# Weight loads of 128 rows of 8 KB, a buffer of its own for w1, and q loads ahead of w2's blocks, in a fused soft-capped attention and maxout kernel

## The chip, the cores and the metric

The kernel runs on one core of one Trainium2 chip, as one launch. The metric is the device time in microseconds (us). Three runs of the kernel before took 338.31, 339.49 and 340.12 us; the median is 339.49 us. The profile is of one execution, recorded by the hardware profiler.

## The reference

Attention over 8 batches of 12 heads, 448 positions, head size 64, with the scores capped by a tanh, then a layer that takes the larger of two projections and projects it back:

```python
scores = cap * np.tanh(scale * np.matmul(q, k.transpose(0, 1, 3, 2)) / cap)
attn = np.exp(scores - max(scores)); attn = attn / sum(attn)
x = (attn @ v).transpose(0, 2, 1, 3).reshape(3584, 768)
h1 = x @ w1            # w1, w2: 768 x 1024, w_out: 1024 x 768
h2 = x @ w2
out = np.maximum(h1, h2) @ w_out
```

All inputs and the output are float32 in HBM.

## The kernel before

The kernel works in bf16 on chip. It rewrites the second layer: max(h1, h2) is h2 + relu(h1 - h2), so the output is x (w2 w_out) + relu(x (w1 - w2)) w_out. Two weight tiles are therefore made on chip in the first 55 us: `wd_sb` = w1 - w2 by six subtractions ("sub", L377), and `wm_sb` = w2 w_out by matmuls ("P", L403) that need w2 turned ("W", 16 or 8 transposes on TensorE at L388, copied to `w2T` at L392 by "WC").

The six row chunks of w1 and w2 are numbered 0 to 5. Chunk 2m + u holds, on partition p, row 256 m + 2 p + u of the matrix. Each chunk is a load of its own, of 128 rows of 4 KB in HBM that lie 8 KB apart. The chunks of w2 go to `w2b`, a view of the buffer that later holds `gT`, and are cast to bf16 on the way ("lw2", L368). The chunks of w1 stay float32 ("lw1", L374): 0 to 3 go to the four output buffers `osb`, 4 and 5 to a view of one of the two `xT` buffers. w_out comes in four quarters `wo_sb` ("lwo half part", L359): `half` picks 384 output columns, `part` picks four of the eight row blocks f.

The work of attention goes by 48 pairs of heads, i = 0 to 47, and two pairs share a step t = i // 2. "lk i", "lq i" and "lv t" load k, q and v (L322 for i under 10, L329 after that, L347 for v); k and q of pair 0 come in on the queues of SP and ACT (L304). For the first ten pairs, TensorE turns q and k ("X", 28 transposes at L430; "XC" copies them out, L435); after that SP does it by DMA transposes ("cr t", L445, `qkT` <- `kqs`). "S i j" are score matmuls (L478), "L t" those of the 64 positions left over (L491); "T", "TL" the tanh and "E", "EL" the exponential on ACT (L483, L495, L499, L502). "Y" and "V" are the sums and the values (L529 to L565), "N" writes `xT` (L574). "M" are the matmuls of the second layer (L598), "ev" evicts them, "st" stores.

Everything is in one hand-written order, the string ORDER, and each engine does its part of it strictly in that order. Loads other than k and q of pair 0 are all issued by POOL and go through one DMA queue. While TensorE has nothing to do at the start, the order gives it "D" steps, a fixed number of 128x128 matmuls on a dummy tile (L441): 29 of them before the first transposes, 8 between "X 1 1" and "S 0 2", one more ahead of "W 2 2", and 17 between "X 2 0" and the first "P". In that stretch TensorE's order is: 29 D, "X" of pair 0, D, S 0 0, S 0 1, X 1, D, S 0 2, D, W 2, W 1, L 0, S 1 0, X 2, 17 D, P 2 (row blocks 0 to 3), P 1 (0 to 3), S 1 1, and so on.

POOL's loads, in order, up to the fourth quarter of w_out: k1, w2 chunk 1, q1, k2, w2 chunk 2, q2, wo 0 0, w2 chunk 0, wo 0 1, q3, q4, k3, four loads of v, k4, w1 chunk 0, wo 1 0, k5, w2 chunk 3, wo 1 1.

Of the kernel before, what the change touches and what calls it, by code (L numbers as in the profile page):

```python
# [14 lines left out]
WC 0; T 1 1; OP 0 0 0; P 0 0 2; T 1 2; P 0 0 1; S 2 0; lk 4 0; P 0 0 1; P 1 0 1; E 1 0 2; P 1 0 1; lw1 0;
S 2 1; P 1 0 2; P 2 0 1; lwo 1 0; P 2 0 1; PC 1 0; P 2 0 2; T 2 0; P 0 0 1; lk 5 0; PC 2 0; X 3 3; lw2 3;
E 1 2 3; P 0 0 1; XC 3; S 2 2; lwo 1 1; P 0 0 2; T 2 1; PC 0 0; lq 5 0; T 2 2; X 4 2; lq 6 0; L 1; lv 1 0;
XC 4; Y 0 1; TL 1; lv 1 1; sub 0 0; V 0 0; E 2 0 3; V 0 1; Y1 0; S 3 0; Y2 0; Y3 0; lv 1 2; OP 0 1 3; P 0 1 1;
T 3 0; N 0 0; P 0 1 3; lv 1 3; N 0 1; OP 2 1 0; P 2 1 2; EL 1; P 2 1 2; S 3 1; S 3 2; T 3 1; OP 1 1 2; P 1 1 2;
lw2 4; W 3 1; P 1 1 1; T 3 2; P 1 1 1; WC 3; S 4 0; E 3 0 2; S 4 1; OP 3 1 1; P 3 1 4; lw2 5; P 0 1 3; T 4 0;  # L20
P 0 1 1; P 1 1 1; lv 2 0; P 1 1 1; PC 0 1; P 1 1 2; E 3 2 3; P 2 1 1; lv 2 1; PC 1 1; S 4 2; X 5 3; lv 2 2;
T 4 1; P 2 1 1; XC 5; P 2 1 1; lv 2 3; P 2 1 1; T 4 2; OP 3 0 2; P 3 0 2; PC 2 1; lw1 4; L 2; Y 1 3; lk 6 0;
TL 2; V 1 0; lk 7 0; Y1 1; E 4 0 3; V 1 1; Y2 1; Y3 1; S 5 0; lq 7 0; N 1 0; W 5 0; lw1 2; W 4 3; N 1 1; T 5 0;
P 3 0 1; WC 5; P 3 0 1; lw1 5; S 5 1; EL 2; P 3 0 1; lw1 1; WC 4; S 5 2; P 3 0 1; lq 8 0; T 5 1; P 3 0 2;
P 3 1 2; PC 3 0; P 3 1 1; T 5 2; lk 8 0; P 3 1 1; OP 4 0 0; P 4 0 1; sub 4 0; P 4 0 3; lk 9 0; E 5 0 2; X 6 3;
PC 3 1; lq 9 0; P 4 0 2; XC 6; P 4 0 2; lw1 3; X 7 2; PC 4 0; S 6 0; XC 7; S 6 1; T 6 0; OP 5 0 1; P 5 0 2;
lv 3 0; sub 2 0; P 5 0 3; E 5 2 3; P 5 0 1; S 6 2; P 5 0 2; T 6 1; OP 4 1 3; P 4 1 1; lv 3 1; sub 5 0; P 4 1 4;
T 6 2; P 4 1 2; L 3; PC 5 0; Y 2 0; lv 3 2; TL 3; V 2 0; sub 1 1; Y1 2; E 6 0 3; V 2 1; Y2 2; Y3 2; S 7 0;
N 2 0; X 8 2; lv 3 3; N 2 1; X 9 1; T 7 0; lq 10 0; XC 8; P 4 1 1; EL 3; S 7 1; XC 9; S 7 2; lq 11 0; OP 5 1 0;
P 5 1 2; PC 4 1; P 5 1 1; T 7 1; P 5 1 1; A 3 0 1; P 5 1 2; lk 10 0; P 5 1 2; T 7 2; sub 3 0; O 0 2; M 0 -1 1;  # L30
lk 10 1; S 8 0; M 0 -1 1; E 7 0 2; M 0 -1 1; S 8 1; PC 5 1; lk 11 0; M 0 -1 2; A 3 0 2; M 0 -1 1; O 1 1;
M 1 -1 1; lk 11 1; M 1 -1 1; H 0; M 1 -1 1; T 8 0; M 1 0 1; A 3 1 1; M 1 0 1; lv 4 0; M 1 0 1; O 2 3; M 2 0 1;
B 3 0; M 2 0 1; E 7 2 3; lv 4 1; S 8 2; M 2 0 1; H 1; B 3 1; M 2 1 1; lv 4 2; M 2 1 1; T 8 1; M 2 1 1; ev 0;
O 3 0; M 3 1 1; lv 4 3; M 3 1 2; T 8 2; H 2; A 3 1 2; M 3 2 2; lk 12 0; cr 5; M 3 2 1; ev 1; O 4 2; M 4 2 1;
L 4; lk 12 1; M 4 2 1; TL 4; Y 3 1; V 3 0; lq 12 0; Y1 3; E 8 0 3; V 3 1; Y2 3; lk 13 0; Y3 3; S 9 0; M 4 2 1;
lv 5 0; N 3 0; M 4 3 2; N 3 1; M 4 3 1; lv 5 1; O 5 1; M 5 3 2; T 9 0; H 4; M 5 3 1; ev 2; lv 5 2; S 9 1;
M 5 4 1; ev 3; M 5 4 1; EL 4; M 5 4 1; lv 5 3; S 9 2; A 4 0 1; O 6 3; M 6 4 2; lk 13 1; M 6 4 1; T 9 1; H 5;
A 4 0 2; M 6 5 3; lq 13 0; ev 4; O 7 0; M 7 5 1; T 9 2; M 7 5 1; S 10 0; H 6; M 7 5 1; M 7 6 1; E 9 0 2;
lk 14 0; M 7 6 1; ev 5; S 10 1; M 7 6 1; O 8 2; M 8 6 1; lk 14 1; M 8 6 1; H 7; M 8 6 1; M 8 7 2; ev 6;
lq 14 0; T 10 0; M 8 7 1; O 9 1; M 9 7 1; A 4 1 1; M 9 7 2; E 9 2 3; lk 15 0; H 8; S 10 2; ev 7; M 9 8 3; cr 6;  # L40
B 4 0; lk 15 1; M 9 8 1; T 10 1; M 9 8 2; B 4 1; M 9 8 2; lq 15 0; T 10 2; M 9 8 2; A 4 1 2; M 9 8 1; O 10 3;
M 10 8 3; L 5; Y 4 0; TL 5; V 4 0; Y1 4; V 4 1; E 10 0 3; Y2 4; Y3 4; S 11 0; M 10 9 1; lv 6 0; N 4 0;
M 10 9 2; M 8 9 1; N 4 1; M 8 9 1; lv 6 1; M 8 9 2; H 10; M 8 9 1; S 11 1; lv 6 2; T 11 0; A 5 0 1; M 8 9 3;
lv 6 3; O 11 0; M 11 9 1; A 5 0 2; EL 5; M 11 9 1; S 11 2; M 11 9 1; lk 16 0; ev 8; M 11 10 2; T 11 1;
M 11 10 1; ev 9; M 11 10 1; cr 7; M 11 10 1; lk 16 1; M 11 10 2; T 11 2; M 11 10 1; S 12 0; lq 16 0; M 11 10 1;
st 0 0; M 11 10 2; E 11 0 2; O 12 2; M 12 10 1; S 12 1; H 11; M 12 10 1; lk 17 0; M 12 10 1; M 12 11 2; H 10 2;
M 12 11 1; lk 17 1; M 10 11 2; H 12; M 10 11 1; T 12 0; A 5 1 1; M 10 11 2; lq 17 0; M 10 11 2; B 5 0;
M 10 11 1; E 11 2 3; O 13 1; M 13 11 1; S 12 2; M 13 11 1; B 5 1; M 13 11 1; M 13 12 1; T 12 1; M 13 12 1;
ev 10; M 13 12 3; lk 18 0; A 5 1 2; T 12 2; M 13 12 3; ev 11; M 13 12 1; lk 18 1; L 6; Y 5 3; TL 6; V 5 0;
lq 18 0; Y1 5; st 0 1; V 5 1; E 12 0 3; Y2 5; lk 19 0; Y3 5; S 13 0; M 13 12 1; lv 7 0; N 5 0; M 13 12 1;  # L50
O 14 0; M 14 12 2; H 13; N 5 1; lv 7 1; M 14 12 1; M 14 13 2; H 12 2; S 13 1; lv 7 2; T 13 0; A 6 0 1;
M 14 13 1; M 12 13 2; lv 7 3; M 12 13 1; H 14; A 6 0 2; EL 6; M 12 13 1; S 13 2; M 12 13 1; lk 19 1; M 12 13 2;
T 13 1; M 12 13 1; O 15 3; M 15 13 1; cr 8; lq 19 0; M 15 13 1; ev 12; M 15 13 1; M 15 14 1; T 13 2; M 15 14 1;
ev 13; S 14 0; M 15 14 1; O 16 2; M 16 14 1; E 13 0 2; M 16 14 1; H 15; S 14 1; M 16 14 1; st 0 2; M 16 15 2;
# [681 lines left out]
```

## Time and profile before

| what | value |
|---|---|
| runs | 338.31, 339.49, 340.12 us |
| span of the profiled execution | 339.5 us (its only time; it equals the median run) |
| TensorE (PE) busy | 327.9 us, 97% of the span |
| ACT busy | 275.3 us, 81% |
| DVE busy | 229.4 us, 68% |
| POOL busy | 169.9 us, 50% |
| DMA packets | 136108, 45.90 MB |
| packets under 512 B / under 2 KB / under 8 KB | 116352 / 131072 / 136064 |
| POOL's load queue (q0) | 96320 packets, 25.08 MB, 76.4% of 16 engines' span |

A packet's size is that of what it writes: the 768 packets of w2 (six chunks of 128 rows) are 2,048 B each, since they are cast to bf16, and the 768 packets of w1 are 4,096 B. The page gives for each engine its busy time; a line of the timeline gives the start, the busy time, the engine, the line of the code, what is written and read, and in brackets the idle time just before it with what ended it. An idle time put down to "issue" is one in which the engine waited for nothing that the profile shows. Times within the span are counted from its first instruction.

### The profile page before, as it was taken

Reading aid. Unit: us, or ns where it says so; the run is one execution under the profiler, and the core shown is the slowest. Engines: PE = TensorE matmul, PEld = TensorE weight load, DVE = VectorE, ACT = ScalarE, POOL = GpSimd, SP = SyncE. Lnnn points to the kernel's source line nnn. Section 1 sums busy time; section 2 is a strip of 40 time slices with the busy share of each in tenths; the row PEclk is TensorE's granted clock in tenths of the full one; section 3 lists DMA queues with packets and bytes.
Section 4 is the critical chain, followed back from the end, with each engine's and each line's share of the span. In section 5 each row is a group of like instructions: output and inputs, shape, how many; then the busy total and the mean of one; then the engine's idle time right before and its main releaser. Section 6 shows DMA issues by size and latency. Waiting matters only on the chain.

```text
span 339.5 us, 9672 instructions
## 1 busy us (share of the span) xinstructions
PE 327.9 (97%) x4076; PEld 194.0 (57%) x4076; DVE 229.4 (68%) x411; ACT 275.3 (81%) x267; POOL 169.9 (50%) x250
## 2 busy tenths in 40 slices
PE   8999999999999999899999999999999999999994
PEld 5644556555767555555655564656565555567662
DVE  2355789786796659667788568856976778774321
ACT  2899989999989998888999998899899999810000
POOL 7476779766674562591871663658737302000000
PEclk9999999999999999999999999999999999999998
DMA  8999999999999999999998999999999963013033
GB/s 144 189 172 188 250 216 99 131 134 183 150 143 129 143 141 113 146 118 132 207 138 84 133 156 190 122 102 220 184 114 126 193 137 48 2 47 95 2 95 93
DMA packets 136108, 45.90 MB, mean 135 GB/s; under 512 B 116352, under 2 KB 131072, under 8 KB 136064
## 3 DMA queue, kind: packets, MB, share of 16 engines
q0 software_dynamic: 96320, 25.08, 76.4%
q1 hardware_dynamic: 39440, 19.86, 33.6%
q8 instruction: 32, 0.52, 0.6%
q10 hardware_dynamic: 304, 0.33, 0.3%
q14 instruction: 12, 0.10, 0.1%
HBM read 47.45 MB, written 11.01 MB: 172 GB/s over the span
## 4 chain that ended last, share of the span: by engine, by line
PE 79%; DMA 7%; DVE 6%; ACT 5%; issue 1%; DVEq 0%
PE mm L598 50%; PE s L478 8%; DMA qkT<-kqs 7%; PE s L561 5%; PE mm L403 4%; ACT e L499 3%; PE mm L441 2%; PE s L491 2%; PE s L565 2%; PE mm L536 2%; PE mm L430 1%; ACT e L483 1%; DVE xT L574 1%; PE mm L388 1%; DVE esum L511 1%
## 5 line engine op out<-in xcount | busy, mean ns | idle before, releaser
L483 ACT ACTIVATE e<-s 128x896 bf16<-128x896 f32 x144 | 127.7, 929 | 6.7 <-PE s L478 6.6
L499 ACT ACTIVATE e<-e 128x2688 bf16<-128x2688 bf16 (+2 forms) x72 | 122.8, 1707 | 0.0
L598 PE MATMUL mm<-wo_sb,gT 64*128 64x384 bf16 x864 | 114.5, 323 | 0.0
L598 PE MATMUL mm<-wm_sb,xT 64*128 64x384 bf16 x648 | 101.0, 323 | 0.0
L598 PE MATMUL mm<-xT,wd_sb 64*128 64x448 bf16 x768 | 99.1, 349 | 0.6 <-DVE gT L619 0.4
L329 POOL DMA_DIRECT2D kqs<-in_k_dram x76 | 54.2, 716 | 71.5 <-DMA qkT<-kqs 71.3
L598 PEld LDWEIGHTS <-gT 64*128 64x128 bf16 x864 | 59.2, 94 | 25.1 <-DVEq L607 0.2
L598 PEld LDWEIGHTS <-wd_sb 64*128 64x128 bf16 x768 | 52.1, 94 | 24.7 <-issue 2.6
L598 PEld LDWEIGHTS <-xT 64*128 64x128 bf16 x648 | 50.4, 94 | 18.6 <-issue 0.6
L478 PE MATMUL s<-qkT 64*128 64x448 bf16 x288 | 56.0, 358 | 3.6 <-DMA qkT<-kqs 1.9
L619 DVE TENSOR_SCALAR gT<-mm 128x448 bf16<-128x448 f32 x64 | 39.6, 622 | 15.0 <-PE mm L598 14.6
L652 DVE COPY osb<-mm 128x384 f32<-128x384 f32 x54 | 29.4, 555 | 25.2 <-PE mm L598 19.8
L511 DVE TENSOR_TENSOR esum<-e 128x896 bf16<-128x896 bf16 x42 | 26.1, 621 | 23.1 <-ACT e L499 16.0
L347 POOL DMA_DIRECT2D vp<-in_v_dram x48 | 30.4, 638 | 22.5 <-PE mm L598 11.1
L329 POOL DMA_DIRECT2D kqs<-in_q_dram x38 | 35.3, 930 | 4.1 <-DMA kqs<-in_k_dram 1.8
L561 PE MATMUL s<-e,vp 128*32 128x448 bf16 x576 | 35.8, 352 | 0.0
L478 PEld LDWEIGHTS <-qkT 64*128 64x128 bf16 x288 | 16.6, 94 | 29.2 <-issue 13.5
L495 ACT ACTIVATE el<-s 128x896 bf16<-128x896 f32 x24 | 22.0, 917 | 13.9 <-PE s L491 13.3
L347 POOL DMA_DIRECT2D vl<-in_v_dram x48 | 29.3, 618 | 6.8 <-DMA wo_sb<-in_moe_w_out_dram 4.1
L662 ACT COPY osb<-mm 128x192 f32<-128x192 f32 x1 | 0.3, 320 | 36.8 <-DMA out_dram<-osb 36.8
L574 DVE TENSOR_TENSOR xT<-s,inv 128x448 bf16<-128x448 f32 x48 | 27.7, 620 | 3.0 <-PE mm L598 0.5
L511 DVE TENSOR_TENSOR esum<-esum,e 128x896 bf16<-128x896 bf16 x42 | 26.2, 624 | 2.2 <-PE mm L598 0.4
(56 smaller groups left out, 272.0 us busy)
## 6 DMA issues: line engine op xcount, KB each, us to landing
out_dram<-osb SPq DMA_DIRECT2D x54, 192.0 KB, 4.8
...
```

Of the source, the lines that this page charges most:

```text
L329: nc.gpsimd.dma_start(out=to, in_=x)
L347: nc.gpsimd.dma_start(out=to, in_=x)
L478: nc.tensor.matmul(s[:, h, :S], k_of(t, o, h, j), q_of(t, o, h))
L483: nc.scalar.activation(expo[i][:, 2 * j : 2 * j + 2, :], slots[i, j][:, :, :S], AF.Tanh, scale=scale / cap)
L495: nc.scalar.activation(left_e[t], slots[t][:, :, :S], AF.Tanh, scale=scale / cap)
L499: nc.scalar.activation(e, e, AF.Exp, scale=float(cap))
L511: nc.vector.tensor_add(d, e[:, 0:2, :] if j == 1 else d, e[:, 2 * j : 2 * j + 2, :])
L561: nc.tensor.matmul(ps[r, u, :S], vp[t % VB][:, m, j if turned_by_pe(t) else 2 * j, u::2], expo[2 * t + o][:, 2 * j + h, :], start=(j == 0) ...
L574: nc.vector.tensor_mul(x, vals[t][:, u, :S], sums[t, 3])
L598: ins = nc.tensor.matmul(self.ps, w[r], x[r], start=first, stop=self.at == [self.n, self.n]).ins
L619: nc.vector.tensor_relu(gT[b // 2][:, f, cs], ps)
L652: nc.vector.tensor_copy(o[:, hs], ps)
```

## The change

Three loads take the place of six for w2, and three the place of six for w1: load c holds chunks 2c and 2c + 1, so each partition gets two neighbouring rows of HBM, 8 KB in one piece. w1 has a buffer of its own, `w1s`, 24 KB on each partition, and no longer uses `osb` and `xT`.

```diff
     def x_rows(w, c):
-        return w.rearrange("(q p u) n -> q u p n", p=P, u=2)[c // 2, c % 2]
+        return w.rearrange("(q p u) n -> q p u n", p=P, u=2)[c]
     def load_w2(c):
-        nc.gpsimd.dma_start(out=w2b[:, c, :], in_=x_rows(moe_w2, c))
+        nc.gpsimd.dma_start(out=w2b[:, 2 * c : 2 * c + 2, :], in_=x_rows(moe_w2, c))
-    w1x = xpool.tile([P, NP, 2 * S], bf16, name="xT").rearrange("p c s -> p (c s)").bitcast(f32)
-    def load_w1(c, eng=nc.gpsimd):
-        w1_in[c] = opool.tile([P, DF], f32, name="osb") if c < OB else w1x[:, (c - OB) * DF : (c - OB + 1) * DF]
-        eng.dma_start(out=w1_in[c], in_=x_rows(moe_w1, c))
+    w1s = const.tile([P, KC, DF], f32, name="w1s")
+    def load_w1(c):
+        for u in range(2):
+            w1_in[2 * c + u] = w1s[:, 2 * c + u, :]
+        nc.gpsimd.dma_start(out=w1s[:, 2 * c : 2 * c + 2, :], in_=x_rows(moe_w1, c))
```

In ORDER only steps lw1 and lw2 move (the rest of the string is wrapped anew). At its start:

```diff
-ld0 k; ld0 q; ms0; lk 1 0; dm; ms; D 3 3; lw2 1; D 3 5; id; D 3 5; lq 1 0; D 3 5; lk 2 0; D 3 5; lw2 2; D 3 2;
-cd k; D 3 1; cd q; D 3 2; lq 2 0; D 3 1; Xh 0 0 0; lwo 0 0; Xh 0 1; XCh 0 0; lw2 0; D 3 1; XCh 0 1; D 3 1;
+ld0 k; ld0 q; ms0; lk 1 0; dm; ms; D 3 3; D 3 5; id; D 3 5; lq 1 0; lw2 0; D 3 5; lk 2 0; D 3 5; D 3 2; cd k; D 3 1;
+cd q; D 3 2; lq 2 0; lw2 1; D 3 1; Xh 0 0 0; lwo 0 0; Xh 0 1; XCh 0 0; D 3 1; XCh 0 1; D 3 1; lwo 0 1; D 3 3; S 0 0;
...
```

Further on, "lw2 3" (behind X 3 3) goes; "lw2 4" becomes "lw2 2" in its place and "lw2 5" goes; "lw1 0" stays where it is (now chunks 0 and 1); "lw1 4" becomes "lw1 2" in its place (chunks 4 and 5); "lw1 2" becomes "lw1 1" in its place (chunks 2 and 3); "lw1 5", "lw1 1" and "lw1 3" go. The loads of POOL, in order, are then: k1, q1, w2 chunks 0 and 1, k2, q2, w2 chunks 2 and 3, wo 0 0, wo 0 1, q3, q4, k3, four loads of v, k4, w1 chunks 0 and 1, wo 1 0, k5, wo 1 1. No step of any engine but POOL moves, and the number of D steps stays.

More of the change, by code (lines that the diff above doesn't have):

```diff
@@ L15 @@
[L15 to L54, printed above, removed]
@@ new lines @@
+P 4 0 2; X 7 2; PC 4 0; S 6 0; XC 7; S 6 1; T 6 0; OP 5 0 1; P 5 0 2; lv 3 0; sub 2 0; P 5 0 3; E 5 2 3; P 5 0 1;
+S 6 2; P 5 0 2; T 6 1; OP 4 1 3; P 4 1 1; lv 3 1; sub 5 0; P 4 1 4; T 6 2; P 4 1 2; L 3; PC 5 0; Y 2 0; lv 3 2; TL 3;
+V 2 0; sub 1 1; Y1 2; E 6 0 3; V 2 1; Y2 2; Y3 2; S 7 0; N 2 0; X 8 2; lv 3 3; N 2 1; X 9 1; T 7 0; lq 10 0; XC 8;
+P 4 1 1; EL 3; S 7 1; XC 9; S 7 2; lq 11 0; OP 5 1 0; P 5 1 2; PC 4 1; P 5 1 1; T 7 1; P 5 1 1; A 3 0 1; P 5 1 2;
+lk 10 0; P 5 1 2; T 7 2; sub 3 0; O 0 2; M 0 -1 1; lk 10 1; S 8 0; M 0 -1 1; E 7 0 2; M 0 -1 1; S 8 1; PC 5 1;
@@ new lines @@
+lk 11 0; M 0 -1 2; A 3 0 2; M 0 -1 1; O 1 1; M 1 -1 1; lk 11 1; M 1 -1 1; H 0; M 1 -1 1; T 8 0; M 1 0 1; A 3 1 1;
+M 1 0 1; lv 4 0; M 1 0 1; O 2 3; M 2 0 1; B 3 0; M 2 0 1; E 7 2 3; lv 4 1; S 8 2; M 2 0 1; H 1; B 3 1; M 2 1 1;
+lv 4 2; M 2 1 1; T 8 1; M 2 1 1; ev 0; O 3 0; M 3 1 1; lv 4 3; M 3 1 2; T 8 2; H 2; A 3 1 2; M 3 2 2; lk 12 0; cr 5;
+M 3 2 1; ev 1; O 4 2; M 4 2 1; L 4; lk 12 1; M 4 2 1; TL 4; Y 3 1; V 3 0; lq 12 0; Y1 3; E 8 0 3; V 3 1; Y2 3;
+lk 13 0; Y3 3; S 9 0; M 4 2 1; lv 5 0; N 3 0; M 4 3 2; N 3 1; M 4 3 1; lv 5 1; O 5 1; M 5 3 2; T 9 0; H 4; M 5 3 1;
@@ new lines @@
+A 5 1 1; M 10 11 2; lq 17 0; M 10 11 2; B 5 0; M 10 11 1; E 11 2 3; O 13 1; M 13 11 1; S 12 2; M 13 11 1; B 5 1;
+M 13 11 1; M 13 12 1; T 12 1; M 13 12 1; ev 10; M 13 12 3; lk 18 0; A 5 1 2; T 12 2; M 13 12 3; ev 11; M 13 12 1;
+lk 18 1; L 6; Y 5 3; TL 6; V 5 0; lq 18 0; Y1 5; st 0 1; V 5 1; E 12 0 3; Y2 5; lk 19 0; Y3 5; S 13 0; M 13 12 1;
+lv 7 0; N 5 0; M 13 12 1; O 14 0; M 14 12 2; H 13; N 5 1; lv 7 1; M 14 12 1; M 14 13 2; H 12 2; S 13 1; lv 7 2;
+T 13 0; A 6 0 1; M 14 13 1; M 12 13 2; lv 7 3; M 12 13 1; H 14; A 6 0 2; EL 6; M 12 13 1; S 13 2; M 12 13 1; lk 19 1;
@@ new lines @@
+ev 52; lq 34 0; Y 13 1; TL 14; V 13 0; Y1 13; lk 35 0; V 13 1; E 28 0 3; Y2 13; Y3 13; lk 35 1; S 29 0; O 55 3;
+M 55 53 1; N 13 0; M 55 53 2; lv 15 0; M 55 54 1; N 13 1; M 55 54 2; lv 15 1; M 55 54 1; ev 53; M 55 54 1; S 29 1;
+T 29 0; M 55 54 1; A 14 0 1; lv 15 2; M 55 54 3; EL 14; M 55 54 1; st 3 3; A 14 0 2; lv 15 3; S 29 2; M 55 54 1;
+O 56 1; M 56 54 2; H 55; lq 35 0; T 29 1; M 56 54 1; M 56 55 1; cr 16; M 56 55 1; H 54 2; M 56 55 1; M 54 55 1;
+T 29 2; M 54 55 1; H 56; S 30 0; M 54 55 3; E 29 0 2; M 54 55 1; S 30 1; M 54 55 2; O 57 2; M 57 55 2; ev 54;
@@ new lines @@
+ev 57; M 59 58 3; A 15 0 2; lk 37 0; T 31 1; M 59 58 2; cr 17; M 59 58 2; lk 37 1; M 59 58 1; T 31 2; O 60 1;
+M 60 58 1; S 32 0; H 59; st 3 5; M 60 58 1; lq 37 0; M 60 58 1; M 60 59 1; E 31 0 2; S 32 1; H 58 2; M 60 59 2;
+M 58 59 2; H 60; M 58 59 4; T 32 0; M 58 59 1; A 15 1 1; M 58 59 1; O 61 2; M 61 59 2; ev 58; E 31 2 3; M 61 59 1;
+S 32 2; B 15 0; M 61 60 3; T 32 1; B 15 1; O 62 0; M 62 60 3; H 61; lk 38 0; ev 59; M 62 61 1; T 32 2; M 62 61 2;
+A 15 1 2; O 63 3; M 63 61 1; lk 38 1; M 63 61 1; H 62; M 63 61 1; ev 60; st 3 6; L 16; lq 38 0; ev 61; M 63 62 1;
@@ new lines @@
+A 16 1 1; M 68 66 2; E 33 2 3; H 67; ev 66; M 68 67 1; S 34 2; M 68 67 1; B 16 0; M 68 67 1; T 34 1; O 69 1;
+M 69 67 2; H 68; B 16 1; M 69 67 1; M 69 68 1; lk 40 0; M 69 68 1; T 34 2; ev 67; M 69 68 3; lk 40 1; M 69 68 1;
+A 16 1 2; M 69 68 4; lq 40 0; L 17; Y 16 0; TL 17; V 16 0; Y1 16; lk 41 0; V 16 1; E 34 0 3; Y2 16; lk 41 1; Y3 16;
+S 35 0; lq 41 0; M 69 68 1; N 16 0; O 70 3; M 70 68 3; H 69; N 16 1; M 70 69 2; lv 18 0; M 70 69 1; H 68 2; S 35 1;
+T 35 0; H 70; A 17 0 1; M 68 69 1; lv 18 1; M 68 69 3; A 17 0 2; M 68 69 1; EL 17; lv 18 2; M 68 69 1; S 35 2;
@@ new lines @@
+cr 21; M 81 80 2; ev 79; O 82 0; M 82 80 1; T 39 2; M 82 80 1; S 40 0; H 81; M 82 80 1; M 82 81 1; E 39 0 2;
+M 82 81 1; ev 80; S 40 1; M 82 81 1; O 83 3; M 83 81 2; H 82; M 83 81 1; M 83 82 2; ev 81; M 83 82 1; T 40 0;
+M 83 82 2; A 19 1 1; M 83 82 2; E 39 2 3; M 83 82 1; S 40 2; B 19 0; M 83 82 3; B 19 1; T 40 1; O 84 2; M 84 82 2;
+lk 46 0; M 84 82 1; H 83; A 19 1 2; M 84 83 2; T 40 2; lk 46 1; M 84 83 1; H 82 2; M 82 83 1; L 20; lq 46 0; Y 19 1;
+TL 20; V 19 0; Y1 19; lk 47 0; V 19 1; E 40 0 3; Y2 19; Y3 19; lk 47 1; S 41 0; M 82 83 1; N 19 0; M 82 83 1; lv 21 0;
@@ new lines @@
+M 82 83 2; N 19 1; M 82 83 2; lv 21 1; M 82 83 1; O 85 1; M 85 83 1; S 41 1; T 41 0; ev 82; M 85 83 1; lv 21 2;
+M 85 83 1; M 85 84 1; A 20 0 1; M 85 84 1; EL 20; M 85 84 1; lv 21 3; S 41 2; ev 83; M 85 84 3; A 20 0 2; lq 47 0;
+T 41 1; M 85 84 2; cr 22; M 85 84 3; T 41 2; O 86 0; M 86 84 1; S 42 0; H 85; M 86 84 1; st 5 3; M 86 84 1; M 86 85 1;
+E 41 0 2; M 86 85 1; H 84 2; S 42 1; M 86 85 1; M 84 85 2; H 86; M 84 85 5; T 42 0; A 20 1 1; M 84 85 1; O 87 3;
+M 87 85 3; ev 84; M 87 86 1; E 41 2 3; M 87 86 1; S 42 2; B 20 0; M 87 86 3; T 42 1; B 20 1; M 87 86 3; ev 85;
@@ new lines @@
+M 87 86 1; T 42 2; M 87 86 2; A 20 1 2; O 88 2; M 88 86 3; H 87; st 5 4; M 88 87 1; L 21; Y 20 1; TL 21; V 20 0;
+Y1 20; V 20 1; E 42 0 3; Y2 20; Y3 20; S 43 0; M 88 87 1; lv 22 0; N 20 0; M 88 87 1; M 86 87 2; H 88; N 20 1;
+M 86 87 1; lv 22 1; M 86 87 3; S 43 1; lv 22 2; T 43 0; A 21 0 1; M 86 87 2; O 89 1; M 89 87 1; lv 22 3; M 89 87 1;
+ev 86; EL 21; M 89 87 1; S 43 2; M 89 88 1; A 21 0 2; M 89 88 2; T 43 1; M 89 88 1; ev 87; M 89 88 1; cr 23;
+M 89 88 3; T 43 2; M 89 88 1; S 44 0; M 89 88 1; st 5 5; M 89 88 1; O 90 0; M 90 88 1; E 43 0 2; M 90 88 1; H 89;
@@ new lines @@
+M 103 101 3; N 23 0; M 103 102 3; N 23 1; M 103 102 4; ev 101; M 103 102 4; O 104 3; M 104 102 2; H 103; st 6 1;
+M 104 102 1; M 104 103 2; H 102 2; M 104 103 1; M 102 103 2; H 104; M 102 103 6; O 105 2; M 105 103 2; ev 102;
+M 105 103 1; M 105 104 2; ev 103; M 105 104 1; O 106 1; M 106 104 2; H 105; M 106 104 1; M 106 105 2; st 6 2; ev 104;
+M 106 105 1; O 107 0; M 107 105 2; H 106; M 107 105 1; M 107 106 2; ev 105; M 107 106 1; O 108 3; M 108 106 2; H 107;
+M 108 106 1; M 108 107 2; ev 106; M 108 107 1; O 109 2; M 109 107 2; H 108; M 109 107 1; M 109 108 2; ev 107;
@@ new lines @@
+M 109 108 1; O 110 1; M 110 108 2; H 109; M 110 108 1; M 110 109 2; ev 108; M 110 109 1; O 111 0; M 111 109 2; H 110;
+M 111 109 1; M 111 110 2; ev 109; M 111 110 1; O 112 3; M 112 110 2; H 111; M 112 110 1; M 112 111 2; ev 110;
+M 112 111 1; O 113 2; M 113 111 2; H 112; M 113 111 1; M 113 112 2; ev 111; M 113 112 9; O 114 1; M 114 112 2; H 113;
+M 114 112 1; M 114 113 2; H 112 2; M 114 113 1; M 112 113 2; H 114; M 112 113 6; O 115 0; M 115 113 2; ev 112;
+M 115 113 1; M 115 114 2; ev 113; M 115 114 7; st 7 3; M 115 114 2; O 116 3; M 116 114 2; H 115; M 116 114 1;
@@ L201 @@
+M 116 115 2; H 114 2; M 116 115 1; M 114 115 2; H 116; M 114 115 6; O 117 2; M 117 115 2; ev 114; M 117 115 1;
+M 117 116 2; ev 115; M 117 116 7; st 7 4; M 117 116 2; M -1 116 2; H 117; M -1 116 1; M -1 117 2; H 116 2; M -1 117 1;
+M 116 117 8; M -1 117 2; ev 116; M -1 117 1; O 118 1; M 118 118 1; ev 117; M 118 118 7; st 7 5; M 118 118 6; O 119 0;
+M 119 119 2; ev 118; M 119 119 12; ev 119; st 7 6;
 """
```

259 lines of the change are left out of this document (114 added, 145 removed).

## The prediction

> **What bounds the kernel now.** I read the page's busy times first, then the busy time by stretches of 10 us, then the chain of work that ended last, then the timeline of TensorE (PE) and of POOL in the first 40 us, and last the packets of POOL's DMA queue.
>
> PE is busy for 327.9 of 339.5 us. By stretches (us, PE, PEld, DVE, ACT, POOL, clock, DMA share, GB/s):
>
> ```profile
> 0.00:10.00 10.00, 8.37 (x96) 5.43 (x97) 2.25 (x14) 3.31 (x4) 7.51 (x17) 1.00 0.85 144
> 10.00:20.00 10.00, 9.34 (x104) 5.86 (x103) 3.12 (x5) 8.46 (x9) 4.90 (x9) 1.00 1.23 184
> 20.00:30.00 10.00, 9.65 (x149) 4.89 (x148) 6.66 (x11) 9.86 (x11) 5.27 (x9) 1.00 1.11 190
> 30.00:40.00 10.00, 9.87 (x133) 5.12 (x129) 6.26 (x12) 10.00 (x11) 7.49 (x14) 1.00 1.14 185
> 130.00:150.00 20.00, 17.45 (x220) 9.40 (x221) 15.49 (x28) 16.67 (x16) 10.06 (x14) 1.00 1.31 130
> ```
>
> From 10 to 40 us PE has 1.1 us of idle time in all, and ACT is full from 20 us on. So a delay of PE there is not absorbed. The waits of PE over the whole span, longest in total first, begin:
>
> ```profile
> PE s L478 <- DMA qkT<-kqs: 1.9, 2, 1.5
> PE mm L441 <- DVE warm L691: 1.1, 1, 1.1
> PE s L478 <- DVE xT L574: 0.8, 3, 0.4
> ```
>
> None is for a load of q, k, v or a weight. What is moved here cannot end a wait of PE, for PE has none there; it can only start one. The one stall of size is the DMA transposes' at 139.08 (the chain of work):
>
> ```profile
> 125.21 13.82 DMA qkT<-kqs
> ```
>
> Why PE needs no load: the D steps stand where it would wait, and they stay. PE's timeline where w2 is first used:
>
> ```profile
> 11.09 0.56 PE L478 MATMUL s<-qkT 64*128 64x448 bf16 x2
> 11.58 0.29 PE L441 MATMUL mm<-warm 128*128 128x128 bf16 x1
> 11.66 1.88 PE L388 MATMUL mm<-ident,gT 128*128 128x128 bf16 x16
> ...
> 14.64 1.34 PE L441 MATMUL mm<-warm 128*128 128x128 bf16 x17
> 15.81 1.46 PE L403 MATMUL mm<-wo_sb,w2T 128*128 128x384 bf16 x8
> ```
>
> "W 2 2" starts at 11.66. POOL's timeline shows when its chunk is there:
>
> ```profile
> 7.68 0.53 POOL L322 DMA_DIRECT2D kqs<-in_q_dram  x1 [0.64 <-DMA gT<-in_moe_w_dram]
> ...
> 10.51 1.25 POOL L347 DMA_DIRECT2D vp<-in_v_dram  x2 [0.86 <-DMA gT<-in_moe_w_dram]
> 13.27 0.59 POOL L347 DMA_DIRECT2D vl<-in_v_dram  x1 [1.51 <-DMA wo_sb<-in_moe_w_out_dram]
> ```
>
> These are POOL's 10th, 13th and 15th loads, held until the 2nd (w2 chunk 1), the 5th (w2 chunk 2) and the 7th (wo 0 0) have landed: each load waits for the one eight before it. So chunk 2 is known to be there at 10.51, 1.15 us before "W 2 2".
>
> **The queue is full.** The DMA view of the first 50 us says of POOL's queue
>
> ```profile
> q0 software_dynamic: 9609, 9.26, 103.6%
> ```
>
> over 100%, since packets overlap. In the packets of the trace the first six loads run back to back from 3.31 us: k1 ends at 4.24, w2 chunk 1 at 7.11, q1 6.99, k2 8.26, w2 chunk 2 at 9.94, q2 10.51, then wo 0 0 at 12.65. What is put ahead of a load therefore delays it by its own length. Packet times (by bytes written): 384 B 51 ns, 768 B 79, 896 B 88, 2,048 B (w2, which reads 4,096 B) 173, 4,096 B (w1) 159; 16 engines take 8 packets each of a load of 128 rows, so a w2 chunk is 8 x 173 = 1.38 us and a w1 chunk 1.27 us.
>
> **Part by part.**
>
> *8 KB rows.* No row shows an 8 KB packet. The four cast sizes lie on a line of 0.073 ns a byte written and 23 ns fixed, so a doubled w2 packet comes to 323 ns, against 2 x 173 = 346: 23 x 8 = 0.18 us saved for each pair of chunks. The ends: 2 x 159 = 318 ns (w1's rate by bytes read) and 346 (nothing saved). I take 323, from the rows of the same kind. All twelve chunks save 1.1 us of queue over 45 us, where PE waits for nothing: worth 0 by itself.
>
> A rule that speaks for the change stands in the Trainium skill, DMA: Bandwidth & Descriptors, "Anatomy of one DMA" (a DMA costs about 2 us fixed plus its bytes) and "Rules for kernel authors" (1 MiB or more per DMA). If that were queue time, six loads fewer would free an estimated 12 us; the seven loads here end one behind the other without such gaps, so the trace shows the fixed part as latency that overlaps, and the sum stays.
>
> *Six POOL issues fewer*, at 0.54 to 0.63 us: 3.4 us of POOL. Worth 0: POOL waits for landings (above), and nobody waits for its issues.
>
> *q1, k2, q2 ahead of w2.* q1 ends near 4.9 instead of 6.99, k2 and q2 near 9.3 instead of 8.26 and 10.51. X 1 (8.80) and X 2 (14.08) start without a wait now, behind PE's own work, so this gains 0 and loses 0.
>
> *w2 chunks ahead of their use.* Now "W 2 2" needs the second block, the sixth load: the old six loads plus two more chunks. 10.51 + 2 x 1.38 - 2 x 0.18 = 12.91. From the last packet to the waiting engine's start took 0.57 us (9.94 to 10.51) and 0.3 us (first k, 3.67, to its cast, 3.97); with 0.4, "W 2 2" starts at 13.3 instead of 11.66: PE **stalls 1.65 us** (1.5 to 2.1 by the ends above). Behind it on PE stand W 1, L 0, S 1 0, X 2, 17 D, P 2, P 1, S 1 1. The tanh of S 1 1 starts at 17.61, 0.04 us after that matmul ends, and ACT is full from there to 44: so ACT takes on the delay.
>
> *The rest of the queue* slips too, less than PE does or with room to spare: wo 0 0 from 12.65 to 15.1 (P 2 at 15.81 + 1.65), wo 0 1 from 16.69 to 17.7 (used near 20.8 + 1.65), v of step 0 from 19.7 to 22 (used at 25.0 + 1.65). Narrowest is wo 1 0: one w2 chunk and one w1 chunk more are ahead of it, 1.38 + 1.27 - 0.55 = 2.1 us; it was seen landed at 26.48 (POOL's next issue), so 28.6, and P 0 1 starts at 26.92, with the delays here (1.65, and 0.4 from below) 28.97. Hidden by 0.4 us; without a delay of PE it would itself stall PE 1.7 us. The two waits are not added: the later takes over what the first does not cost. From k5 on the order has the old amount ahead of it, and then less.
>
> *w1's own buffer.* No wait in the trace names a w1 load as a buffer's user, and the subtractions end by 55 us, before the first output eviction: 0. *w1 chunks 2 and 3 together, earlier*: DVE never waits for a w1 load: 0.
>
> *PE's clock.* A 128x128x128 matmul takes 311 ns until 13.3 us (W at L388) and 219 ns from 14.6 (D): PE runs slower until about 13.4, where 11.66 to 13.5 is its first dense stretch. If the switch follows the dense stretch, it moves with W at no cost; if it comes at a fixed time, W itself runs faster, -0.6 us; if it comes later, X 2 takes 0.89 instead of 0.56 us (as X 1 did) and the 17 D 0.142 instead of 0.067 us each (the chain has 5 D in 0.71 us at 1.62 and 15 in 1.00 at 14.98), +1.6. I take +0.4, between the first and the last.
>
> **Sum:** 339.5 + 1.65 + 0.4 = **341.5 us**, against the profile's 339.5 and the median of 339.49. Under 0.5% (1.7 us, about what a measurement can tell) counts as no change, so this is just beyond it.
>
> **The rivals.**
>
> 1. *The clock comes a window later* (slower). For: the stall falls into the stretch that switched it. Price: the full 1.6 instead of 0.4, and the P matmuls behind partly slow: 342.7 to 343.5. Against: W alone may be enough. The Trainium skill, TensorE: Matmul & The Clock Gate, Part 1, gives half rate until about 3.4 us of sustained activity, in windows that run freely, and calls the phase variable from run to run; the two durations above agree, the length of the window no run here shows.
>
> 2. *The transposes' wait at 139 goes* (no change). PE stood 1.5 us there. That transfer ran beside loads of v and stores, and took 13.82 us where the page's median is 7.1; shifting everything by 2 us may part them. 341.5 - 1.5 to 2 = 339.5 to 340. Against: the loads and the issue of the transposes follow PE, so they shift together, and another one may collide.
>
> 3. *No stall* (not slower): larger packets move bytes so much faster that the second block is there in time. It decides at 10.51 - 2.77 + 16 p + 0.4 = 11.66, p = 220 ns a packet. Then 339.5, or 337.8 if the wait at 139 goes as well. Against: w1's packets need 159 ns for half the bytes read. If the rows are cut into 4 KB again, this is out, and the stall is 2.0.
>
> **How the numbers follow.** Forecast 0.45 (most of it beyond 1.7 us: slower 0.36, same 0.09); rival 1 0.20, slower; rival 2 0.17 (same 0.15, faster 0.02); rival 3 0.10 same, and 0.08 faster with the wait at 139 gone. Slower 0.56, same 0.34, faster 0.10. The range is from 339.2 (rivals 2 and 3, less what lies below) to 343.5 (rival 1).
>
> **What would show it.** Packets: 135,340 in all, and 134,912 under 8 KB. In PE's timeline W 2 2 near 13.3 with an idle time of about 1.6 us released by gT's load; ACT idle as long before the tanh of S 1 1; PE's 10 to 20 us near 7.7 busy; no wait at P 0 1. The 17 D at 0.067 or 0.142 us tell of the clock. Wrong would be: W 2 2 without a wait, P 0 1 waiting for wo_sb on top, or the difference sitting behind 130 us.

## The result and the profile after

| | before | after |
|---|---|---|
| median of 20 runs each | 339.39 us | 341.06 us |
| lowest and highest run | 338.27 to 343.5 | 338.8 to 342.33 |
| the profiled run, its span | not timed by itself, 339.5 us | 338.8 us, 336.9 us |
| PE busy | 327.9 us | 327.0 us |
| POOL busy (instructions) | 169.9 us (250) | 166.8 us (244) |

The ratio of the times is 1.0041, with an interval of 1.0025 to 1.0057: 1.4 us slower (the two medians lie 1.7 us apart). That is a loss, but the ratio is below the 0.5% that was named as the bound, and the interval contains that bound. Here and below a ratio leaves out runs over 1.5% above the fastest of their kernel: the 343.5 us of before, two runs of "w2's half" (345.03 and 345.54, the second of which is the profiled one) and one of "fewer D" (343.21).

The two spans go the other way (336.9 after, 339.5 before), and that is the first thing to read rightly. Wherever one run has both numbers, its time is 1.7 to 1.9 us above its span (338.8 and 336.9 here, 340.96 and 339.1 or 339.47 and 337.7 in the second profiles further down). So the profiled run of before took about 341.3 us, 1.9 us over its median, and the profiled run of after is the fastest of its 20. **The statement ahead of the prediction that the profiled execution of before equals the median run took a span for a time, and was wrong.** These two profiles must not be subtracted from each other. A second profile of each kernel, taken in the experiments, came from runs near the medians (339.47 and 340.96 us), and the reading below rests on those.

After's page: its packets, POOL's queue (packets, MB, share of 16 engines), and the loads of w1 (KB each, median us from issue to landing):

```profile
DMA packets 135244, 45.90 MB, mean 136 GB/s; under 512 B 116256, under 2 KB 130976, under 8 KB 134816
...
q0 software_dynamic: 95456, 25.08, 76.3%
...
w1s<-in_moe_w_dram POOLq DMA_DIRECT2D x3, 1024.0 KB, 7.7
```

The change does what it says: 864 packets fewer than before, where 768 were expected (the other 96 are small ones, of under 512 B), and 1,248 fewer under 8 KB: the same 96, 384 of w2's, and w1's 768, which are now 384 of 8 KB. In the packets of the trace a w2 packet of 4,096 B written takes 324 ns (323 was forecast), and one of w1 of 8,192 B 309 ns, where two of 4,096 B take 318.

PE's timeline of after where w2 is first used (start, busy time, and in brackets the idle time ahead with what ended it):

```profile
11.59 0.23 PE L430 MATMUL mm<-warm 128*128 128x128 bf16 x1
12.18 1.07 PE L377 MATMUL mm<-ident,gT 128*128 128x128 bf16 x16 [0.36 <-DMA gT<-in_moe_w_dram]
...
14.34 1.34 PE L430 MATMUL mm<-warm 128*128 128x128 bf16 x17
15.52 1.46 PE L392 MATMUL mm<-wo_sb,w2T 128*128 128x384 bf16 x8
```

The same lines of the second profile of after:

```profile
10.98 0.23 PE L430 MATMUL mm<-warm 128*128 128x128 bf16 x1
12.82 1.68 PE L377 MATMUL mm<-ident,gT 128*128 128x128 bf16 x16 [1.61 <-DMA gT<-in_moe_w_dram]
...
16.33 1.40 PE L430 MATMUL mm<-warm 128*128 128x128 bf16 x17
17.57 0.65 PE L392 MATMUL mm<-wo_sb,w2T 128*128 128x384 bf16 x3
```

And of the second profile of before:

```profile
11.58 0.29 PE L441 MATMUL mm<-warm 128*128 128x128 bf16 x1
11.66 1.91 PE L388 MATMUL mm<-ident,gT 128*128 128x128 bf16 x16
...
15.12 1.34 PE L441 MATMUL mm<-warm 128*128 128x128 bf16 x17
16.30 1.46 PE L403 MATMUL mm<-wo_sb,w2T 128*128 128x384 bf16 x8
```

The line with `ident,gT` is "W 2 2". Before, it has no bracket: PE comes to it and goes on. After, it has one in both profiles, and what ended the idle time is the load of w2, as forecast. Between the two runs near the medians the whole loss can be followed: W starts 1.16 us later (12.82 against 11.66), the first P 1.27 us later (17.57 against 16.30), a given matmul near 100 us 1.37 us later (102.03 against 100.66, from the instructions of the trace), and the spans differ by 1.4 us (339.1 against 337.7). So nearly all of it is there at the first P. ACT takes the delay over where it was said to, at the tanh of S 1 1; here it is in the second profiles of before and of after:

```profile
18.09 1.77 ACT L483 ACTIVATE e<-s 128x896 bf16<-128x896 f32 x2 [0.56 <-PE s L478]
```

```profile
19.37 1.77 ACT L472 ACTIVATE e<-s 128x896 bf16<-128x896 f32 x2 [1.73 <-PE s L467]
```

The first profile of after shows how a shorter wait (0.36 us) can cost nothing. Its W took 1.07 us instead of 1.91, since PE's clock had already gone up when it started, and its first P came at 15.52, 0.78 us ahead of 16.30; its span is 0.8 us shorter. The lines of the stretch from 10 to 20 us (us, PE, PEld, DVE, ACT, POOL, clock, DMA share, GB/s), first after, then after again, then before again:

```profile
10.00:20.00 10.00, 8.98 (x105) 5.19 (x103) 3.04 (x5) 8.55 (x9) 4.17 (x8) 1.00 1.24 185
```

```profile
10.00:20.00 10.00, 8.23 (x96) 5.41 (x95) 2.52 (x5) 6.83 (x7) 5.08 (x10) 0.83 1.25 191
```

```profile
10.00:20.00 10.00, 9.34 (x102) 5.72 (x100) 3.12 (x5) 7.98 (x9) 5.01 (x9) 1.00 1.23 182
```

The column behind POOL's is the granted clock. In after again it is 0.83: the clock record of the trace has it up at 9.67, back down at 13.09, in the middle of W, and up again at 16.5. The column doesn't show the slow stretch before the first rise (W ran slow in before again too, at 1.00); the durations do. The steps from 9.67 to 13.09 and to 16.5 are 3.4 us each. The Trainium skill, TensorE: Matmul & The Clock Gate, Part 1, speaks of free-running windows of about 3.4 us whose phase differs from run to run; this run's record agrees with the length, and the three runs with the phase.

The stretch of the DMA transposes, 130 to 150 us, in before again:

```profile
130.00:150.00 20.00, 18.85 (x238) 10.19 (x236) 16.48 (x30) 18.23 (x19) 12.79 (x19) 1.00 1.34 134
```

PE is busy for 18.85 us where the first profile of before had 17.45. The 1.9 us for which that profile's PE waited for `qkT` stand in no list of waits of before again, of after or of after again: in this size they were that one execution's (two of the experiments show 0.5 us).

### The profile page after: what moved, and what is told of

It reads as the page before. It is cut to its first block, busy times and chain, and to the rows that moved or that the text cites. A ratio compares the mean times of both kernels' runs of the same rounds, so it can differ in the third digit from the quotient of the medians.

```text
span 336.9 us, 9664 instructions
## 1 busy us (share of the span) xinstructions
PE 327.0 (97%) x4076; PEld 193.3 (57%) x4076; DVE 229.4 (68%) x411; ACT 274.8 (82%) x267; POOL 166.8 (49%) x244
## 4 chain that ended last, share of the span: by engine, by line
PE 77%; ACT 7%; DVE 6%; DMA 5%; issue 2%; POOL 1%; POOLq 0%; DVEq 0%
PE mm L587 51%; PE s L467 8%; PE s L550 6%; PE mm L392 4%; ACT e L488 4%; DMA gT<-in_moe_w_dram 2%; PE s L480 2%; ACT e L472 2%; PE s L554 2%; PE mm L525 2%; DMA qkT<-kqs 2%; DVE xT L563 1%; PE mm L419 1%; DVE esum L505 1%; PE mm L377 1%
```

## The experiments

The expectations name the theory of the prediction A: the second block of w2 comes later than PE's "W 2 2", and PE's clock follows. Other letters are rivals that put the loss elsewhere; D, formed after the first four, is a clash of subtractions: POOL now comes to its own w1 - w2 some 4 us earlier (42.48 instead of 46.71 in the first two profiles), and while both engines subtract, DVE's takes far longer. All were timed in five rounds against the kernel before, with 12 runs each unless another number is given.

**Before and after again.** No edit.

> The kernel before, once more, for a second profile. Its time is within 0.3 us of the other runs of before. If the waits that only the first profile of before has (PE 1.7 us at 136 to 139 us and 0.6 at 220 to 225, for DMA transposes) belong to the kernel, they are there again; if they are chance, one or both are gone, and the profile's span is 337 to 338 us.

Measured 339.4 us, ratio 0.9978 (0.9949 to 1.0008), which also shows how far a kernel can lie from itself here.

> The changed kernel once more, for its time on the chip of this call and another profile. 1.0 to 1.9 us above before. Theory A: the profile shows a wait of 0.4 us or more at W 2 2 and no other stall before 55 us that before lacks. Theory D: besides that it shows, in about half of such profiles, a subtraction of DVE of 2 to 3.2 us beside POOL's between 41 and 46 us and PE waiting 1 to 1.7 us for the qkT copy behind it.

Measured 340.79 us, ratio 1.0046 (1.0018 to 1.0073). The loss is confirmed. Both profiles were read above.

**Each half alone.** w1's half: before, with the three w1 loads of 8 KB rows into `w1s`.

```diff
-lw1 0; ... lw1 4; ... lw1 2; ... lw1 5; ... lw1 1; ... lw1 3;
+lw1 0; ... lw1 2; ... lw1 1;
```

> Before, with the w1 half of the change alone: three w1 loads of 128 rows of 8 KB into a buffer of their own; w2 and the order of k, q and w2 as before. Theory A (PE waits at W 2 2 for the second w2 block, and the rest of the loss follows from that): W 2 2 starts near 11.66 us without a wait, time within 0.5 us of before. Theory B (the loss comes from w1: 24 KB more on each partition, or the bigger w1 load ahead of wo 1 0, which would make P 0 1 wait near 27 us): 1 to 1.7 us slower than before, with a wait at P 0 1 or a difference behind 55 us. Theory C (rows of 8 KB move worse, or disturb the queue): 0.5 us or more slower.

Measured 340.22 us, ratio 1.001 (0.9989 to 1.003); W starts at 11.67 without a wait, and the span is 337.5. The buffer of its own and the larger w1 loads are worth nothing that can be measured here, where the interval goes from 0.4 us faster to 1.0 slower.

w2's half: before, with the three w2 loads and q1, k2 and q2 as in after, w1 as in before.

```diff
-D 3 3; lw2 1; D 3 5; id; D 3 5; lq 1 0; D 3 5; lk 2 0; D 3 5; lw2 2; D 3 2;
+D 3 3; D 3 5; id; D 3 5; lq 1 0; lw2 0; D 3 5; lk 2 0; D 3 5; D 3 2;
...
```

> Before, with the w2 half of the change alone: three w2 loads of 8 KB rows, q1, k2, q2 placed as in the changed kernel; w1 in six loads in osb and xT as before. Theory A: the whole loss, 1.0 to 1.9 us slower than before, W 2 2 starting 0.5 us or more after S 0 2 and its D end, waiting for gT's load. Theory B: within 0.5 us of before. Theory C: about half of the loss, 0.7 us.

Measured 340.3 us, ratio 1.0015 (0.9992 to 1.0038), which falls short of the 1.0 to 1.9 us expected and settles nothing in time. Its runs spread widely (338.5 to 345.54), and the profile is of the longest, so it shows a place and not a typical size. Its line shows how far the wait can go:

```profile
15.56 1.89 PE L386 MATMUL mm<-ident,gT 128*128 128x128 bf16 x16 [3.79 <-DMA gT<-in_moe_w_dram]
```

In its packets the last eight, one engine's share of the second block, end at 15.18, some 3 us behind the rest of the block, and PE starts 0.38 us after that. A part of this delay can be seen: that engine's packets stop from 12.26 to 13.11, and one packet of 16,384 B of the instruction queue runs from 12.24 to 13.13. The profile of "fewer D" below has the same pair (12.35 to 13.20, and 12.33 to 13.22). The records do not name the engine, so this is read from the times alone, and the larger part of the delay lies before it.

**The first block first.** In after, chunks 0 and 2 change places in W, WC, OP, P and PC, so that PE's first use needs the first block. Nothing else moves.

```diff
-W 2 2; ... WC 2; ... OP 2 0 1; P 2 0 3; ... W 0 3; ... WC 0; ...
+W 0 2; ... WC 0; ... OP 0 0 1; P 0 0 3; ... W 2 3; ... WC 2; ...
```

> The changed kernel, with w2's chunks 0 and 2 exchanged in the steps that turn w2 and multiply it by w_out (W, WC, OP, P, PC), so that the two chunks turned first both lie in the first w2 block; loads as in the changed kernel. Theory A: no wait at the first W (its block ends near 8.2 us of the span), and the time goes back to that of before, 0 to 0.5 us faster or slower than before. Theory B and theory C: no difference to the changed kernel, 1 to 1.7 us slower than before.

Measured 340.63 us, ratio 1.0036 (1.0011 to 1.0061). The wait is gone (W at 11.66, P at 15.75), and yet hardly any time is won. Its timelines, DVE, POOL and then PE:

```profile
41.51 3.23 DVE L372 TENSOR_TENSOR wd_sb<-w1s,gT 128x1024 bf16<-128x1024 f32 x1
```

```profile
41.48 2.16 POOL L372 TENSOR_TENSOR wd_sb<-w1s,gT 128x1024 bf16<-128x1024 f32 x1
```

```profile
45.79 0.55 PE L473 MATMUL s<-qkT 64*128 64x448 bf16 x4 [1.62 <-DVE qkT L430]
```

A subtraction of DVE takes 1.21 to 1.22 us by itself. This one starts beside POOL's and takes 3.23; the copy of the transposed q and k behind it on DVE comes late, and PE waits 1.62 us: what the exchange had won is given back 30 us later. The Trainium skill, SBUF — State Buffer, "SBUF: two separate sides", has DVE operations with two inputs in SBUF and GpSimd's (POOL's) share a pair of ports by a lock that is held for a whole instruction. By that rule DVE's 1.22 us would begin when POOL's operation ends, at 43.64, and end at 44.86; the trace has 44.74.

**POOL's subtraction elsewhere.** After, and the kernel of the exchange, each with "sub 1 1" (on POOL) later.

```diff
-V 2 0; sub 1 1; Y1 2; ... lk 10 0; P 5 1 2;
+V 2 0; Y1 2; ... lk 10 0; sub 1 1; P 5 1 2;
```

> The changed kernel with POOL's subtraction (sub of chunk 1, 2.1 us) moved behind POOL's load of k10, some 4 us later. Theory D (POOL waits less, so its subtraction comes 4 to 5 us earlier than before and runs at the same time as a subtraction of DVE, which then takes 3.2 instead of 1.2 us and makes PE wait 1.6 us in some of the runs): all five subtractions of DVE take 1.22 us, POOL's starts after 46.9 us, and the time is 0.5 to 1.2 us less than that of the changed kernel, 0.2 to 0.9 us above before. Theory A (all of the loss is the wait at W 2 2 and what follows): no difference to the changed kernel.

> The changed kernel with both: w2's chunks 0 and 2 exchanged (no wait at the first W) and POOL's subtraction behind k10. Theory D and A together: both waits gone, the time within 0.5 us of before (339.4 to 339.7 in the shared runs), PE's start times within 0.3 us of before's up to 55 us. If a loss of 1 us or more stays, there is a third cause that neither theory has.

Measured 342.28 us, ratio 1.0062 (1.0035 to 1.0089), and 342.0 us, ratio 1.0062 (1.0039 to 1.0084). Both missed: the move made a clash in the place of none, or another in the place of the first. DVE and POOL of the one from after:

```profile
46.66 5.52 DVE L372 TENSOR_TENSOR wd_sb<-w1s,gT 128x1024 bf16<-128x1024 f32 x2
```

```profile
48.95 2.14 POOL L372 TENSOR_TENSOR wd_sb<-w1s,gT 128x1024 bf16<-128x1024 f32 x1
```

Two subtractions that take 2.35 us elsewhere take 5.52 (the second alone 4.39), and PE waits 1.7 us for `xT` behind them. Here DVE's second one is recorded from 47.8, ahead of POOL's, and is held up all the same, by 3.2 us where POOL's operation took 2.14. By that rule of the Trainium skill the one that starts first keeps the ports and would lose nothing. The two profiles of before agree: there DVE's starts 0.76 and 0.62 us ahead of POOL's and takes 1.22, and POOL's takes 2.46 and 2.61. Here the trace differs, and it decides; why is open. In each of the seven profiles where DVE's was held it ended 1.1 us behind POOL's, so a recorded start need not be the start of its work. With the exchange the same wait is there, and on top the granted clock was 0.83 from 50 to 60 us (it fell from 53.4 to 56.8). So the times of this pair do not tell of the wait at W, although the first P starts at 15.39 with the exchange and at 17.65 without.

**No subtraction on POOL at all.** "sub 1 0" instead of "sub 1 1" puts chunk 1's on DVE, in the same place; once in after, once with the exchange.

```diff
-V 2 0; sub 1 1; Y1 2;
+V 2 0; sub 1 0; Y1 2;
```

> The changed kernel with the subtraction of chunk 1 given to DVE (1.22 us there, in a gap of 1.25 us ahead of the sums of step 2) instead of POOL, so that POOL and DVE never subtract at the same time; the wait at W 2 2 stays. Theory D alone (the clash of the two subtractions is the loss): within 0.5 us of before. Theory A, now with a spread (W 2 2 was 0.5, 0.6, 1.1 and 3.9 us late in four profiles, and the clock's switch moves with it): 1 to 1.7 us slower than before, as the changed kernel is, and PE 0.5 us or more behind before from W 2 2 on.

> The same, and w2's chunks 0 and 2 exchanged, so that the first two W find their chunks in the first w2 block: neither wait nor clash. Theory A: 1 us or more faster than the kernel with the subtraction on DVE alone, within 0.4 us of before, PE within 0.5 us of before up to 136 us. Theory D: the same as the kernel with the subtraction on DVE alone.

Measured 341.73 us, ratio 1.006 (1.003 to 1.009), and 340.05 us, ratio 1.0019 (0.9995 to 1.0044). This is the pair that decides: neither has a clash, and they differ by the exchange alone. The means of their twelve runs are 341.89 and 340.14, 1.7 us apart, 0.9 either way by the spread of the runs. Against before the first is some 2 us slower, where 1 to 1.7 was expected. PE's line at the first W in both (the first profile is of a long run, 343.46 us):

```profile
14.23 1.89 PE L383 MATMUL mm<-ident,gT 128*128 128x128 bf16 x16 [2.36 <-DMA gT<-in_moe_w_dram]
```

```profile
11.67 1.91 PE L383 MATMUL mm<-ident,gT 128*128 128x128 bf16 x16
```

**Rows of 4 KB under the new order.** After, each load cut in two, so that there are also six more loads for POOL to issue.

```diff
-        nc.gpsimd.dma_start(out=w2b[:, 2 * c : 2 * c + 2, :], in_=x_rows(moe_w2, c))
+        for u in range(2):
+            nc.gpsimd.dma_start(out=w2b[:, 2 * c + u, :], in_=x_rows(moe_w2, c)[:, u])
...
-        nc.gpsimd.dma_start(out=w1s[:, 2 * c : 2 * c + 2, :], in_=x_rows(moe_w1, c))
+            nc.gpsimd.dma_start(out=w1s[:, 2 * c + u, :], in_=x_rows(moe_w1, c)[:, u])
```

> The changed kernel with each 8 KB-row load issued as two loads of 4 KB rows at the same place of the order (12 weight loads again, w1 still in its own buffer). Theory A: by the packet times 2 x 0.18 us more queue ahead of W 2 2, so its wait is 0.3 to 0.5 us longer than in the changed kernel, and the time 0.3 us longer, 1.5 to 2.2 us slower than before. Theory C: faster than the changed kernel by 0.5 us or more. Theory B: the same as the changed kernel.

Measured 342.18 us (six runs), ratio 1.0085 (1.0062 to 1.0109), the highest ratio of all. The lines of PE:

```profile
12.26 1.89 PE L378 MATMUL mm<-ident,gT 128*128 128x128 bf16 x16 [0.39 <-DMA gT<-in_moe_w_dram]
...
29.56 1.46 PE L393 MATMUL mm<-wo_sb,w2T 128*128 128x384 bf16 x8 [1.18 <-DMA wo_sb<-in_moe_w_out_dram]
```

The wait at W is no longer than with 8 KB rows. But it is there, although "W 2 2" needs only chunk 2 now, which lands at 12.21 (chunk 3 at 14.68): the order alone, with chunks 0 and 1 and the loads of q and k ahead, brings a wait. And now wo 1 0 is late for P 0 1: it lands at 29.52, in the two profiles of after at 26.31 and 24.96. So under this order the three larger loads of each matrix are worth 1.1 to 1.4 us (342.18 against the two medians of after), and not at W, but 17 us later. That it is the size of the packets is not shown, and only a small part can be: by the packet times the two w2 blocks and the w1 block ahead of wo 1 0 save 0.4 us (2 x 0.18 + 0.07). POOL issues wo 1 0 at 20.62 instead of 18.75 and 18.44, behind three more loads and behind landings that it waits for, so most of what is seen goes with the number of loads.

**Looking for a faster one.** The kernel of "exchange and later subtraction" without the 8 D steps between X 1 and S 0 2:

```diff
-D 3 2; XC 1; D 3 3; T 0 1; D 3 3; S 0 2;
+XC 1; T 0 1; S 0 2;
```

> The kernel with both cures, less the eight D between X 1 and S 0 2 (1.4 us of dummy matmuls). ACT is full from 11.7 to 44 us, so an S 0 2 that comes 1.4 us earlier lets ACT start its full stretch 1.4 us earlier; the first w2 block lands near 8.5 us, so the first W can start at 10.2. Expected: 0.7 to 1.4 us faster than the kernel with both cures, 338.0 to 339.0, if no load is late; wo 1 0 (landed near 25.6) is then needed at 25.5 and may cost 0.1 to 0.5. With the loads of before this would wait for w2 (landed at 10.5). If the clock switches later for it, nothing is gained.

Measured 339.66 us, ratio 0.9986 (0.9964 to 1.0008): as fast as before, and 2.3 us faster than with the D steps. PE waits after all, for the load of the first block and for w_out:

```profile
PE mm L398 <- DMA wo_sb<-in_moe_w_out_dram: 0.8, 1, 0.8
...
PE mm L383 <- DMA gT<-in_moe_w_dram: 0.5, 1, 0.5
```

Its clash is gone too (POOL's subtraction starts at 49.41), and so is the fall of the clock near 53 us, so how much of the 2.3 us is whose stays open. Last, the exchange with all subtractions on DVE, 5 D steps fewer, wo 1 0 ahead of the first w1 load, and the first subtraction later:

```diff
-D 3 2; XC 1; D 3 3; T 0 1; D 3 3; S 0 2; ... lw1 0; ... lwo 1 0; ... sub 0 0; V 0 0; ... N 0 1;
+XC 1; D 3 3; T 0 1; S 0 2; ... lwo 1 0; ... lw1 0; ... V 0 0; ... N 0 1; sub 0 0;
```

> The kernel with neither wait nor clash, less five of the eight D between X 1 and S 0 2 (0.9 us), wo 1 0 issued ahead of the first w1 load, and DVE's subtraction of chunk 0 moved behind N 0 (out of the way of the sums of step 0, where PE waits 0.35 us for xT). Expected 0.8 to 1.4 us faster than the kernel with neither wait nor clash: 338.0 to 338.8 where before has 339.4. If a load comes late on one of the 16 DMA engines, or the clock's switch moves behind the first W, half of it goes.

Measured 340.0 us, ratio 1.0011 (0.9985 to 1.0038): a miss. P starts early (14.98), but a subtraction waits 1.7 us for w1, and PE behind it 1.9 us for `xT` at 52.98; the clock fell from 53.6 to 57.0. No version beats before by more than its interval.

**The account over the profiles.** From the first P on PE does the same matmuls in every kernel, so a span can be worked out from the start of the first P and the waits behind it that before again lacks. Against its 16.30 and 337.7:

| kernel | P starts | against 16.30 | later waits of PE | sum | span less 337.7 |
|---|---|---|---|---|---|
| before, first profile | 15.81 | -0.49 | `qkT` 1.9 | +1.4 | +1.8 |
| w1 alone | 16.13 | -0.17 | | -0.2 | -0.2 |
| after, first profile | 15.52 | -0.78 | | -0.8 | -0.8 |
| after again | 17.57 | +1.27 | | +1.3 | +1.4 |
| first block | 15.75 | -0.55 | clash 1.6 | +1.1 | +1.1 |
| rows of 4 KB | 17.21 | +0.91 | `wo_sb` 1.2 | +2.1 | +2.3 |
| subtraction later | 17.65 | +1.35 | clash 1.7 | +3.1 | +3.2 |
| first block, subtraction later | 15.39 | -0.91 | clash 1.7 | +0.8 | +2.2 |
| fewer D | 17.59 | +1.29 | | +1.3 | +1.3 |
| after, subtractions on DVE | 19.51 | +3.21 | `xT`, `wd_sb` 0.5 | +3.7 | +4.0 |
| first block, subtractions on DVE | 15.96 | -0.34 | `qkT`, `xT`, `wd_sb` 1.0 | +0.7 | +1.1 |
| the last one above | 14.98 | -1.32 | `xT`, `e` 2.0 | +0.7 | +2.3 |
| w2 alone (its longest run) | 21.28 | +4.98 | `qkT` 0.5 | +5.5 | +6.1 |

The two kernels whose clock fell near 53 us (the exchange with the later subtraction, and the last one) lose 1.4 and 1.7 us more than that sum: the stretch from 50 to 60 us of the first of them is (columns as above)

```profile
50.00:60.00 10.00, 8.29 (x99) 4.66 (x99) 8.70 (x16) 8.36 (x9) 6.40 (x10) 0.83 1.26 116
```

One profile of each kernel is little, but several kernels share their beginning. Up to the first P, w1 alone does what before does, and the two kernels of after with the subtraction later or on DVE do what after does. In the three profiles that begin as before the first P starts at 15.81, 16.13 and 16.30, and in the four that begin as after at 15.52, 17.57, 17.65 and 19.51. The means are 1.5 us apart (16.08 and 17.56), which is the loss in time. With the exchange it starts at 15.75, 15.39 and 15.96.


## Why the prediction was right, and where it was not

**The step that decided held.** "W 2 2" needs the second block, waits for it, and PE's delay is absorbed nowhere. The exchange in the pair without a clash takes it away; in w1's half alone W has no such wait. The first sign that was named, an idle time at W released by gT's load, is in all six profiles where W uses the second block, and none is at P 0 1 in after. The sum of the change, +2.05, was too large: +1.4 to +1.7 us. By the bound of the prediction itself, 0.5%, the ratio of 0.41% more lies on the side of no change, to which it gave 0.34, though the interval (0.25 to 0.57%) reaches past the bound: the way was right, and the size that it needed to call it slower is not shown. PE's 10 to 20 us were put at 7.7 busy; they are 8.98 and 8.23.

**The stall was sized too high.** Predicted were 1.65 us; in the four profiles that begin as after W starts 0.52, 0.63, 1.16 and 2.57 us behind 11.66, 1.2 on average. The packet time was right (324 ns for 323), and so were the 0.4 us from the last packet to PE (0.34 to 0.38 here). What failed is the start of the sum, the 10.51 at which the six old loads ended, taken as loads that run back to back. By the prediction's own packet times they need 5.6 us from 3.31, to 8.9; they ended at 10.51, and at 10.30 in before again, with nine and ten w2 packets of over 600 ns, up to 1,664. So some 1.5 us that the packet times do not give were in the base. The same working for after gives 11.35 for the second block, and its last packet, predicted at 12.91, ended at 11.83 and 12.48. The range of 1.5 to 2.1 was also far too narrow: over the profiles with the wait W starts from 12.18 to 15.56, since one late engine of 16 can decide. Why one is late was found only in small part (the instruction packet above).

**The clock** was put at +0.4 between -0.6 and +1.6. From W to the first P took 4.15, 4.46 and 4.64 us in the three profiles that begin as before, and 3.34, 4.75, 5.28 and 5.36 in the four that begin as after: +0.3 on average. Against the 4.15 of the profile that the prediction started from these are -0.8 to +1.2, so the end below was a little small. Rival 1, the full 1.6, was seen once, in the longest run of w2 alone (5.72), and in no profile of after. The reason given, that W is PE's first dense stretch, does not hold: the timeline of that profile lists no idle time of PE from 1.07 us to W, and in both profiles of after the clock rose (11.56 and 9.67) before W started. The wait does move the clock, though. It is up to stay at 12.5 to 14.7 us in the six profiles with the full D steps and no wait at W, and at 11.56 and 16.1 to 21.7 in the six with that wait.

**The base and rival 2.** That the two first profiles differ behind 130 us was named as a sign of being wrong; the second profiles lack it. The 339.5 us that the sum starts from is a span, of a run of about 341.3 us; it came out at the median's number by chance, so the forecast of 341.5 stayed near 341.06. Rival 2 took the wait for the transposes at 139 us as part of the kernel. In that size it was that execution's alone, the profiles near the medians lack it, and there was no saving to be had from its going.

**Rival 3** (no stall) would need p under 220 ns; 324 rules it out.

**The 8 KB rows, "worth 0 by itself".** The packet times agree with that (0.4 us of queue ahead of wo 1 0), but the larger loads as such are worth 1.1 to 1.4 us under this order. The prediction had put wo 1 0 2.1 us later, seen landed at 28.6, 0.4 us ahead of its use, with the larger loads. It hardly moved: it landed at 26.31 in after and 26.19 in before, at 24.96 and 25.26 in the second profiles. In the first profile of after that is 0.3 us ahead of P 0 1 (26.62), and with twice as many loads it is the one that makes PE wait. A cost hidden by 0.4 us should have been kept in the sum as a bound.

**Six issues fewer, "worth 0",** was right in the sum for after but missed what they do, on both sides. With the issues back, as in rows of 4 KB, wo 1 0 is issued some 2 us later and PE does wait for it. And without them POOL comes to its subtraction 4 us earlier. In after that meets DVE's only briefly (1.63 instead of 1.22 us in after again), in four of the experiments fully, at 1.6 to 1.7 us of PE in three of them.
